# Clustered attention and a routed expert layer on one core: column groups, joint transposes, and sums moved off TensorE

## The chip, the cores and the metric

The kernel runs on one core of one Trainium2 chip. A core has TensorE (PE, matrix multiply; its weight loads are a row of their own, PEld), VectorE (DVE), ScalarE (ACT), GpSimd (POOL) and the queues that start transfers (SP is the queue of SyncE). The metric is the time of one execution on the device in microseconds (us). Before the change it is 852.24 us, the median of three runs (851.85 to 852.52).

## The reference

Two layers follow each other. The first is attention in clusters: queries and keys are assigned to the nearest of 16 centroids of their head, and a query sees only keys of its own cluster. The second sends each of 3072 rows to the one expert of 8 with the highest logit.

```python
# q, k, v: (4, 8, 768, 64); centroids: (8, 16, 64)
q_assign = argmax(q_n . c_n);  k_assign = argmax(k_n . c_n)          # per head
mask   = q_assign[:, :, :, None] == k_assign[:, :, None, :]
scores = where(mask, q @ k.T / sqrt(64), -1e9)
attn   = exp(scores - max);  attn = attn / (sum(attn) + 1e-9)
x      = (attn @ v) as rows (3072, 512)
# experts: w_gate (512, 8), w1 (8, 512, 1024), w2 (8, 1024, 512)
logits = x @ w_gate;  e = argmax(logits);  g = softmax(logits)[e]
out    = g * (relu(x @ w1[e]) @ w2[e])
```

## The kernel before

The kernel works on head pairs: 4 batches x 4 pairs = 16. A pair's queries and keys are turned (`turn`), compared with the centroids (`similar`, `similar2`), assigned (`assign`, `assign2`: one-hot rows), and the one-hots are turned too (`put`), so that a matmul of one-hots adds 0 where clusters agree and a huge negative number where they don't. Then come 12 units of scores and attention (`score`, `attend`) in two turns of six. Later `weigh` sums the exponentials and multiplies the attention result by the gate's matrix, `weigh2` turns both, `x_turn` writes the rows. The expert stage runs one group of rows per expert: whole tiles of 128 rows and one of 32.

```python
def put(g):                                       # one-hots of pair g, q and k apart
    ohT[g] = ohp.tile([P, 2, S], BF16, name="ohT")
    ps = ps_s.tile([P, 2, 512], F32, name="sps").bitcast(BF16)
    for w in range(2):
        for j in range(NQ):
            nc.tensor.transpose(  # L651
                ps[:, w, j * P : (j + 1) * P],
                ohs[:, (j % (NQ // 2)) * 4 + w * 2 + j // (NQ // 2)].rearrange("p a c -> p (a c)"), ident_b,
            )
    nc.scalar.copy(ohT[g][:, 0, :], ps[:, 0, 0:S])  # L655
    nc.vector.tensor_scalar(ohT[g][:, 1, :], ps[:, 1, 0:S], scalar1=BIG, scalar2=-BIG, op0=ALU.mult, op1=ALU.add)  # L656

def score(u):
    g, half, j = where(u)
    qs = slice(half * HS, (half + 1) * HS)
    ks = slice(j * P, (j + 1) * P)
    ps = ps_s.tile([P, 2, 512], F32, name="sps")
    for a in range(2):
        r = slice(a * D, (a + 1) * D)
        nc.tensor.matmul(ps[:, a, 0:HS], lhsT=qk[g][r, 1, ks], rhs=qk[g][r, 0, qs], start=True, stop=False)  # L673
    for a in range(2):
        r = slice(a * D, (a + 1) * D)
        nc.tensor.matmul(ps[:, a, 0:HS], lhsT=ohT[g][r, 1, ks], rhs=ohT[g][r, 0, qs], start=False, stop=True)  # L676
    A[u] = ap.tile([P, 2, HS], F32, name="A")
    nc.scalar.activation(A[u], ps[:, :, 0:HS], AF.Exp)  # L678

def weigh(g):                                     # sums and logits, two column groups of 32
    ps = ps_m.tile([P, 512], F32, name="mps")
    t = [T.pop((g, half)) for half in range(2)]
    for i in range(3):
        for half in range(2):
            nc.tensor.matmul(  # L711
                ps[half * 32 : (half + 1) * 32, 0:HS],
                lhsT=one_row[:, i, :] if i < 2 else wg[:, g % HP, :],
                rhs=t[half][:, i, :] if i < 2 else XT[g][:, half * HS : (half + 1) * HS],
                start=(i == 0), stop=(i == 2),
            )
    lsT[g] = stat.tile([64, HS], F32, name="lsT", bufs=1)
    nc.scalar.copy(lsT[g], ps[0:64, 0:HS])  # L718

def weigh2(g):
    lt = lsT.pop(g)
    ps = ps_m.tile([P, 512], F32, name="mps")
    for i in range(NQ // 2):
        nc.tensor.transpose(ps[:, i * 64 : (i + 1) * 64], lt[:, i * P : (i + 1) * P], ident[0:64, 0:64])  # L725
    ls = stat.tile([P, NQ, 32], F32, name="ls")
    nc.vector.tensor_copy(ls, ps[:, 0 : NQ * 32].rearrange("p (t r) -> p t r", r=32))  # L727
    den = ls[:, :, 2 * E : 2 * E + 2]
    # ...
```

The scaling in `turn`, and the order in which the parts stand (of a turn, part 0 comes between its six scores and its six attends, part 1 behind the attends; the scores of pair g begin in turn n = 2 g):

```python
def turn(g, piece):
    # ... transposes of queries and keys into ps (L599)
    if piece == 0:
        nc.vector.tensor_scalar_mul(flat[:, 0:S], ps[:, 0:S], D**-0.5)  # L603
        nc.scalar.copy(flat[:, S:1024], ps[:, S:1024])  # L604
    else:
        nc.scalar.copy(flat[:, 1024 : 2 * S], ps[:, 0 : 2 * S - 1024])  # L606

for g in range(NG):
    n = g * TG
    if g == 0:
        at(-4, 0, turn, g, 0)
        at(-4, 1, turn, g, 1)
        at(-3, 0, similar, g)
        at(-3, 1, similar2, g)
    elif g == 1:
        for f, a in ((turn, (g, 0)), (turn, (g, 1)), (similar, (g,)), (similar2, (g,))):
            at(-1 if f is similar2 else -2, 1, f, *a)
    else:
        at(n - 3, 0, turn, g, 0)
        at(n - 3, 0, turn, g, 1)
        at(n - 3, 1, similar, g)
        at(n - 2, 0, similar2, g)
    at(n - 2, 0, assign, g)
    at(n - 2, 0, assign2, g)
    at(n - 1, 0, put, g)
    at(n, 1, finish, g, 0)
    at(n + 1, 1, finish, g, 1)
    # ...
```

`similar` holds L613 (matmuls with the centroids) and L618, `similar2` L624 and L626, `assign` and `assign2` L632 to L641, `attend` L693, `finish` L701 (its result `xT`), `x_turn` L754 and L757.

The experts' second layer. The 32 rows use four column groups, each over a quarter of the 1024 inner elements, and a last matmul with `fold` (four identities of 32 on top of each other) adds the four parts; `rows_out` scales (L315) and scatters (L316) the rows. The first layer is L301, its evictions L309 and L311; L282 turns gathered rows.

```python
def layer2(g):
    zq = zc = None
    if g["n"][last] < P:
        zq = wide()
        n = FB * RQ // P
        for i in range(n):
            for t in range(P // RQ):
                nc.tensor.matmul(  # L334
                    zq[t * RQ : (t + 1) * RQ, 0, :], lhsT=g["h"][:, t * n + i, last * P : last * P + RQ],
                    rhs=g["w"][1][:, t * n + i, :], start=(i == 0), stop=(i == n - 1),
                )
        zc = p1.tile([P, Dm], F32, name="zo", bufs=3)
        nc.vector.tensor_copy(zc, zq[:, 0, :])  # L339
    for j, m in enumerate(g["n"]):
        if m < P:
            continue
        zp = wide()[:, 0, :]
        for fb in range(FB):
            nc.tensor.matmul(  # L345
                zp, lhsT=g["h"][:, fb, j * P : (j + 1) * P], rhs=g["w"][1][:, fb, :],
                start=(fb == 0), stop=(fb == FB - 1),
            )
        rows_out(g, j, P, zp)
    if zc is not None:
        zf = wide()[0:RQ, 0, :]
        nc.tensor.matmul(zf, lhsT=fold, rhs=zc, start=True, stop=True)  # L352
        rows_out(g, last, RQ, zf)
```

At the end two questions are loaded and asked: whether more groups of rows are left than were unrolled, and whether the general path has to run. With these inputs neither does.

```python
nx = nc.values_load(xe[0:1, NX : NX + 1], min_val=0, max_val=NX)  # L1020
general = nc.values_load(xe[0:1, NX + 1 : NX + 2], min_val=0, max_val=1)  # L1021
with tc.If(nx > XU):  # L1022
    with tc.For_i(XU, nx, 1) as i:
        ex = nc.sync.value_load(xe[0:1, bass.ds(i, 1)], min_val=0, max_val=E - 1)
        # ...
mctx.close()
late.close()
with tc.If(general > 0):  # L1035
    in_general(tc, ident, ident_b, first_c, first_e, wpool, q, k, v, centroids, moe_w_gate, moe_w1, moe_w2, out)
```

Of the kernel before, what the change touches and what calls it, by code (L numbers as in the profile page):

```python
# [8 lines left out]
F32 = mybir.dt.float32  # L9
# [12 lines left out]
XU = 2  # L22
# [161 lines left out]
def kernel(  # L184
# [78 lines left out]


    def wide():
        return ps_s.tile([P, 2, 512], F32, name="sps")
# [46 lines left out]
    def rows_out(g, j, m, zp):  # L313
        zo = p1.tile([P, Dm], F32, name="zo", bufs=3)
# [10 lines left out]
    def layer2(g):  # L325
        last = len(g["n"]) - 1
        zq = zc = None
        if g["n"][last] < P:

            zq = wide()  # L330
            n = FB * RQ // P
            for i in range(n):
                for t in range(P // RQ):
                    nc.tensor.matmul(  # L334
                        zq[t * RQ : (t + 1) * RQ, 0, :], lhsT=g["h"][:, t * n + i, last * P : last * P + RQ],
                        rhs=g["w"][1][:, t * n + i, :], start=(i == 0), stop=(i == n - 1),
                    )
            zc = p1.tile([P, Dm], F32, name="zo", bufs=3)
            nc.vector.tensor_copy(zc, zq[:, 0, :])  # L339
# [10 lines left out]
        if zc is not None:  # L350
            zf = wide()[0:RQ, 0, :]
            nc.tensor.matmul(zf, lhsT=fold, rhs=zc, start=True, stop=True)  # L352
            rows_out(g, last, RQ, zf)
# [7 lines left out]
    fold = consts.tile([P, RQ], F32)  # L361
# [5 lines left out]
    def place_consts():  # L367
# [9 lines left out]

        for t in range(P // RQ):
            nc.gpsimd.tensor_copy(fold[t * RQ : (t + 1) * RQ, :], ident[t * RQ : (t + 1) * RQ, t * RQ : (t + 1) * RQ])
# [22 lines left out]
    xe = rte.tile([1, NX + 2], I32)  # L402
# [100 lines left out]
    with ExitStack() as actx:  # L503
        ld = actx.enter_context(tc.tile_pool(name="ld", bufs=2))
        qkp = actx.enter_context(tc.tile_pool(name="qkp", bufs=2))
        ohp = actx.enter_context(tc.tile_pool(name="ohp", bufs=2))
# [37 lines left out]
        nc.vector.tensor_copy(ident_b, ident)  # L544
        first_c = iota("first_c", [P, C], [[-1, C]], C, 0)
        first_e = iota("first_e", [P, E], [[-1, E]], E, 0)

        wg = consts.tile([P, DB, 32], F32)
        nc.gpsimd.memset(wg, 0.0)
        one_row = consts.tile([P, 2, 32], F32)  # L550
        nc.gpsimd.memset(one_row, 0.0)
        for a in range(2):
            r = slice(a * D, (a + 1) * D)
            nc.gpsimd.tensor_copy(wg[r, :, a * E : (a + 1) * E], wg_in[r])
            nc.gpsimd.memset(one_row[:, a, 2 * E + a : 2 * E + a + 1], 1.0)

        ohs = consts.tile([P, 2 * NQ, 2, D], BF16, name="oh")
        nc.gpsimd.memset(ohs, 0.0)

# [31 lines left out]
        def turn(g, piece):  # L591
# [9 lines left out]
            if piece == 0:  # L601

                nc.vector.tensor_scalar_mul(flat[:, 0:S], ps[:, 0:S], D**-0.5)  # L603
# [33 lines left out]
        def assign2(g):  # L637
# [3 lines left out]
            nc.vector.tensor_tensor(  # L641
                ohs[:, :, :, 0:C], rank.rearrange("p (t a) c -> p t a c", a=2),
                top.rearrange("p (t a) -> p t a", a=2).unsqueeze(3).to_broadcast([P, 2 * NQ, 2, C]), op=ALU.is_equal,
            )

        def put(g):
            ohT[g] = ohp.tile([P, 2, S], BF16, name="ohT")
            ps = ps_s.tile([P, 2, 512], F32, name="sps").bitcast(BF16)
            for w in range(2):
                for j in range(NQ):  # L650
                    nc.tensor.transpose(  # L651
                        ps[:, w, j * P : (j + 1) * P],
                        ohs[:, (j % (NQ // 2)) * 4 + w * 2 + j // (NQ // 2)].rearrange("p a c -> p (a c)"), ident_b,
                    )
            nc.scalar.copy(ohT[g][:, 0, :], ps[:, 0, 0:S])  # L655
            nc.vector.tensor_scalar(ohT[g][:, 1, :], ps[:, 1, 0:S], scalar1=BIG, scalar2=-BIG, op0=ALU.mult, op1=ALU.add)  # L656
# [49 lines left out]
        def weigh(g):  # L706
            ps = ps_m.tile([P, 512], F32, name="mps")
            t = [T.pop((g, half)) for half in range(2)]
            for i in range(3):
                for half in range(2):  # L710
                    nc.tensor.matmul(  # L711
                        ps[half * 32 : (half + 1) * 32, 0:HS],
                        lhsT=one_row[:, i, :] if i < 2 else wg[:, g % HP, :],
                        rhs=t[half][:, i, :] if i < 2 else XT[g][:, half * HS : (half + 1) * HS],
                        start=(i == 0), stop=(i == 2),
                    )
            lsT[g] = stat.tile([64, HS], F32, name="lsT", bufs=1)
            nc.scalar.copy(lsT[g], ps[0:64, 0:HS])  # L718

        def weigh2(g):  # L720
# [3 lines left out]
            for i in range(NQ // 2):  # L724
                nc.tensor.transpose(ps[:, i * 64 : (i + 1) * 64], lt[:, i * P : (i + 1) * P], ident[0:64, 0:64])  # L725
            ls = stat.tile([P, NQ, 32], F32, name="ls")
            nc.vector.tensor_copy(ls, ps[:, 0 : NQ * 32].rearrange("p (t r) -> p t r", r=32))  # L727
            den = ls[:, :, 2 * E : 2 * E + 2]
# [3 lines left out]

            lgh = stat.tile([P, NQ, 2, E], F32, name="lgh")
            nc.vector.tensor_tensor(
                lgh, ls[:, :, 0 : 2 * E].rearrange("p t (a e) -> p t a e", a=2),
# [59 lines left out]
        for g in range(NG):  # L795
# [6 lines left out]
            elif g == 1:  # L802

                for f, a in ((turn, (g, 0)), (turn, (g, 1)), (similar, (g,)), (similar2, (g,))):
                    at(-1 if f is similar2 else -2, 1, f, *a)
# [107 lines left out]
    with tc.tile_pool(name="sm", bufs=1) as sm:  # L913
# [54 lines left out]
        xe_f = sm.tile([1, NX + 2], F32)  # L968
# [7 lines left out]
        nc.vector.tensor_tensor(xe_f[:, NX : NX + 1], ove[0:1, E - 1 :], bad[0:1, 3:4], op=ALU.mult)  # L976
# [88 lines left out]
```

## Time and profile before

| | |
|---|---|
| median of three runs | 852.24 us |
| span in the profile | 849.3 us |
| mean granted TensorE clock | 0.995 |
| instructions | 10767 |
| attention: scores begin to be complete | 22.83 us |
| one head pair, in the steady part | 24.8 us |
| expert stage with gathered rows, first matmul | 467.89 us |
| last matmul starts | 837.70 us |

A profile is one execution. Its page gives the busy time of each engine, the chain of work that ended last, and groups of instructions: source line, engine, operation, output <- inputs, shape, how often, busy time, mean ns of one, and the idle time just before them with what ended it. The timeline gives the same instructions in order of time: start, length, engine, line, how many were merged, and in brackets the idle time of the engine before them. Line numbers are those of the kernel before. A 32-bit matmul stands there as two records; a 32-bit transpose and a bf16 matmul as one. The length of a matmul's record includes time in the pipeline, so two neighbours overlap; what a block of matmuls costs is the distance from its start to the start of the next block.

In the stages, of 100 us from 200 to 300 (attention) PE is busy 100.0, DVE 65.2, ACT 52.9 and POOL 5.4; of 100 us from 600 to 700 (experts) PE 100.0, DVE 8.9, ACT 12.0 and POOL 15.9.

### The profile page before, as it was taken

The numbers are of one execution on the slowest core, as the hardware profiler recorded it, in microseconds if no ns is written. First come the engines' busy times: TensorE is split into PE (matmuls) and PEld (weight loads), VectorE is DVE, ScalarE is ACT, GpSimd is POOL, SyncE is SP. The second block draws the span as 40 slices with busy tenths as digits, with TensorE's granted clock in tenths as the row PEclk, the third lists the DMA queues.
The fourth block names the chain that finished last, engine by engine and source line by source line (L and its number), as shares of the span: only waits on it lengthen the run. The fifth ranks groups of instructions, "written<-read, shape, count | busy, mean of one in ns | idle before, by whom it ended". The sixth has DMA issues, their size and how long they took to land.

```text
span 849.3 us, 10767 instructions
## 1 busy us (share of the span) xinstructions
PE 820.6 (97%) x4397; PEld 435.6 (51%) x4397; DVE 320.5 (38%) x559; ACT 264.0 (31%) x406; POOL 106.2 (13%) x165
## 2 busy tenths in 40 slices
PE   4999999999999999999999999999999999999994
PEld 2544455454455555454666655645454444545472
DVE  3566666675666566786452101001001010101000
ACT  3554555555455455545311111111011111110010
POOL 2200000000000000011024020211020303020010
PEclk9999999999999999999999999999999999999998
DMA  9027321272242102201332243443242424321010
GB/s 206 1 57 239 72 56 56 77 254 56 57 131 57 37 21 57 94 1 39 137 150 63 73 173 137 150 163 117 112 140 112 166 100 160 119 69 70 25 39 7
DMA packets 76186, 81.69 MB, mean 96 GB/s; under 512 B 52831, under 2 KB 56927, under 8 KB 75616
## 3 DMA queue, kind: packets, MB, share of 16 engines
q1 hardware_dynamic: 70208, 60.82, 23.6%
q0 software_dynamic: 5248, 20.04, 6.4%
q8 instruction: 37, 0.61, 0.3%
q14 instruction: 21, 0.17, 0.1%
q10 hardware_dynamic: 672, 0.05, 0.1%
HBM read 68.26 MB, written 13.68 MB: 96 GB/s over the span
## 4 chain that ended last, share of the span: by engine, by line
PE 48%; issue 39%; POOL 8%; DVE 3%; ACT 1%; DMA 0%; POOLq 0%; ACTq 0%; DVEq 0%
PE sps L673 14%; PE O L693 14%; PE mps L711 4%; PE sps L676 3%; POOL out_dram L316 3%; POOL xg L270 3%; PE sps L599 2%; PE sps L613 2%; PE sps L754 2%; PE sps L301 2%; PE sps L651 1%; POOL oh_c L468 1%; PE sps L624 1%; PE sps L345 1%; DVE T L685 1%
## 5 line engine op out<-in xcount | busy, mean ns | idle before, releaser
L301 PE MATMUL sps<-xgT,w 128*128 128x416 f32 (+2 forms) x640 | 175.2, 434 | 1.1 <-ACT xgT L290 1.1
L678 ACT ACTIVATE A<-sps 128x768 f32<-128x768 f32 x192 | 153.1, 811 | 50.2 <-PE sps L676 48.9
L345 PE MATMUL sps<-w,h_sb 128*128 128x512 f32 x368 | 160.6, 595 | 1.3 <-DVE h_sb L309 0.9
L673 PE MATMUL sps<-qk 64*128 64x384 f32 x768 | 158.6, 491 | 0.0
L301 PEld LDWEIGHTS sps<-xgT,w 128*128 128x128 f32 x640 | 111.1, 190 | 67.5 <-issue 49.8
L309 DVE TENSOR_SCALAR h_sb<-sps 128x416 f32<-128x416 f32 (+2 forms) x34 | 18.7, 550 | 316.6 <-PE sps L301 316.6
L693 PE MATMUL O<-A,v_in 128*64 128x384 f32 x768 | 130.9, 490 | 0.0
L685 DVE TENSOR_TENSOR T<-T,A 128x768 f32<-128x768 f32 x128 | 122.7, 958 | 13.8 <-DVE T L681 0.5
L345 PEld LDWEIGHTS sps<-w,h_sb 128*128 128x128 f32 x368 | 69.1, 190 | 91.7 <-issue 85.6
L673 PEld LDWEIGHTS sps<-qk 64*128 64x128 f32 x768 | 66.6, 187 | 47.7 <-issue 41.2
L693 PEld LDWEIGHTS O<-A,v_in 128*64 128x64 f32 x768 | 52.3, 137 | 62.7 <-issue 62.6
L315 ACT ACTIVATE zo<-sps,xg 128x512 f32<-128x512 f32 (+1 forms) x34 | 23.3, 685 | 180.0 <-PE sps L345 171.0
L316 POOL DMA_INDIRECT out_dram<-zo,s_idx x34 | 33.0, 969 | 319.0 <-ACT zo L315 316.1
L311 ACT ACTIVATE h_sb<-sps 128x416 f32<-128x416 f32 (+2 forms) x34 | 16.5, 485 | 162.7 <-DVE h_sb L309 162.7
L676 PE MATMUL sps<-ohT 64*128 64x384 bf16 x384 | 63.2, 323 | 0.3 <-DVE ohT L656 0.3
L634 POOL TENSOR_TENSOR sim<-sim,first_c 128x384 f32<-128x384 f32 x16 | 16.0, 998 | 270.3 <-DVE sim L633 270.3
L681 DVE SCALAR_TENSOR_TENSOR T<-A 128x768 f32<-128x768 f32 x32 | 30.6, 958 | 49.0 <-ACT A L678 49.0
L701 ACT COPY xT<-O 128x384 f32<-128x384 f32 x32 | 15.4, 483 | 73.6 <-PE O L693 73.6
L270 POOL DMA_INDIRECT xg<-x_rows,g_idx x34 | 32.8, 964 | 20.1 <-issue 9.8
L676 PEld LDWEIGHTS <-ohT 64*128 64x128 bf16 x384 | 19.3, 94 | 25.5 <-DVE ohT L656 0.9
L757 DVE TENSOR_TENSOR x<-sps,rd 128x384 f32<-128x384 f32 x32 | 17.6, 553 | 28.4 <-PE sps L754 28.4
L711 PE MATMUL mps<-T,one_row 128*32 128x384 f32 x128 | 23.8, 492 | 0.0
(191 smaller groups left out, 534.0 us busy)
## 6 DMA issues: line engine op xcount, KB each, us to landing
w<-in_moe_w_dram SPq DMA_DIRECT2D x20, 2048.0 KB, 8.8
x_rows<-x POOLq DMA_DIRECT2D x4, 1548.0 KB, 7.2
q_in<-in_q_dram SPq DMA_DIRECT2D x32, 192.0 KB, 4.5
k_in<-in_k_dram SPq DMA_DIRECT2D x32, 192.0 KB, 4.7
v_in<-in_v_dram SPq DMA_DIRECT2D x16, 384.0 KB, 3.3
xg<-x_rows,g_idx POOLq DMA_INDIRECT x34, 5.5
out_dram<-zo,s_idx POOLq DMA_INDIRECT x34, 2.9
csb<-in_centroids_dram ACTq DMA_DIRECT2D x1, 32.0 KB, 1.7
```

Of the source, the lines that this page charges most:

```text
L270: nc.gpsimd.indirect_dma_start(out=g["xg"][0:m, j, :], out_offset=None, in_=x_d[0 : g["rows"], :], in_offset=bass.IndirectOffsetOnAxis(ap= ...
L301: nc.tensor.matmul(o, lhsT=g["w"][0][:, c, fb * P : (fb + 1) * P], rhs=g["xT"][:, c, :cols], start=(c == 0), stop=(c == DB - 1),)
L315: nc.scalar.activation(zo[0:m], zp[0:m], AF.Copy, scale=g["xg"][0:m, j, Dm : Dm + 1])
L316: ins = nc.gpsimd.indirect_dma_start(out=out[:, :], out_offset=bass.IndirectOffsetOnAxis(ap=g["si"](j)[0:m], axis=0), in_=zo[0:m], in_offs ...
L345: nc.tensor.matmul(zp, lhsT=g["h"][:, fb, j * P : (j + 1) * P], rhs=g["w"][1][:, fb, :], start=(fb == 0), stop=(fb == FB - 1),)
L673: nc.tensor.matmul(ps[:, a, 0:HS], lhsT=qk[g][r, 1, ks], rhs=qk[g][r, 0, qs], start=True, stop=False)
L676: nc.tensor.matmul(ps[:, a, 0:HS], lhsT=ohT[g][r, 1, ks], rhs=ohT[g][r, 0, qs], start=False, stop=True)
L678: nc.scalar.activation(A[u], ps[:, :, 0:HS], AF.Exp)
L681: nc.vector.scalar_tensor_tensor(T[g, half], in0=A[u - 1], scalar=1e-9 / P, in1=A[u], op0=ALU.add, op1=ALU.add)
L685: nc.vector.tensor_tensor(T[g, half], T[g, half], A[u], op=ALU.add)
L693: nc.tensor.matmul(O[g, half][a * D : (a + 1) * D, 0:HS], lhsT=rows[g, "v"][:, a, j, :], rhs=a_[:, a, :], start=(j == 0), stop=(j == NQ - 1),)
L711: nc.tensor.matmul(ps[half * 32 : (half + 1) * 32, 0:HS], lhsT=one_row[:, i, :] if i < 2 else wg[:, g % HP, :], rhs=t[half][:, i, :] if i ...
```

## The change

Five things are changed at once.

1. Sums and logits in four column groups. `weigh` used three matmuls for each of two column groups, with both heads' sums and logits in the same 32 columns. Now each half and head has a column group of its own, with two matmuls. The result fills 128 partitions instead of 64.
2. Joint one-hot transposes. Queries' and keys' one-hots stand side by side in 128 columns, so one transpose turns both: 6 instead of 12. The keys' part is then taken from other partitions by two operations on 16 partitions each. Rows that no key fills are set to 0 once, in two fixed buffers.
3. The 32-row sums leave TensorE: `fold` and its matmul go; ScalarE copies three of the four parts, VectorE adds them.
4. One question at the end: a value computed earlier says whether either of the two paths is needed.
5. Another order of the first turns: pair 1's similarities come a turn later, so that they no longer stand before pair 0's one-hot transposes, ScalarE scales pair 1's queries, and 12 matmuls of the identity run at the start, before any data is there.

```diff
 def layer2(g):
...
+            zc = pools["wk"].tile([RQ, P // RQ, Dm], F32, name="zc", bufs=1)
+            for t in range(1, P // RQ):
+                nc.scalar.copy(zc[:, t, :], zq[t * RQ : (t + 1) * RQ, :])
+            nc.vector.tensor_tensor(zc[:, 0, :], zc[:, 1, :], zq[0:RQ, :], op=ALU.add)
+            for t in range(2, P // RQ):
+                nc.vector.tensor_tensor(zc[:, 0, :], zc[:, 0, :], zc[:, t, :], op=ALU.add)
+            rows_out(g, last, RQ, zc[:, 0, :])
...
-        if zc is not None:
-            zf = wide()[0:RQ, 0, :]
-            nc.tensor.matmul(zf, lhsT=fold, rhs=zc, start=True, stop=True)
-            rows_out(g, last, RQ, zf)
...
-        for t in range(P // RQ):
-            nc.gpsimd.tensor_copy(fold[...], ident[...])
...
+        ps = ps_m.tile([P, 512], F32, name="mps")
+        for i in range(12):
+            nc.tensor.matmul(ps[:, 0:P], lhsT=ident, rhs=ident, start=True, stop=True)
...
-        ohs = consts.tile([P, 2 * NQ, 2, D], BF16, name="oh")
+        ohs = ohp.tile([P, NQ, 2, 2, 32], BF16, name="oh")
         nc.gpsimd.memset(ohs, 0.0)
+        ohTs = []
+        for i in range(2):
+            t = ohp.tile([P, 2, S], BF16, name=f"ohT{i}")
+            nc.gpsimd.memset(t[:, 1, :], 0.0)
+            ohTs.append(t)
...
 def turn(g, piece):
-                nc.vector.tensor_scalar_mul(flat[:, 0:S], ps[:, 0:S], D**-0.5)
+                if g == 1:
+                    nc.scalar.mul(flat[:, 0:S], ps[:, 0:S], D**-0.5)
+                else:
+                    nc.vector.tensor_scalar_mul(flat[:, 0:S], ps[:, 0:S], D**-0.5)
...
 def assign2(g):                                  # the comparison is cut in two, for q and for k
...
 def put(g):
+            oh = ohT[g] = ohTs[g % 2]
+            ps = wide()[:, 0, :].bitcast(BF16)
+            for j in range(NQ):
+                nc.tensor.transpose(
+                    ps[:, j * P : (j + 1) * P],
+                    ohs[:, (j % (NQ // 2)) * 2 + j // (NQ // 2)].rearrange("p a w c -> p (a w c)"), ident_b,
+                )
+            nc.scalar.copy(oh[:, 0, :], ps[:, 0:S])
+            for a in range(2):
+                nc.vector.tensor_scalar(
+                    oh[a * D : a * D + C, 1, :], ps[a * D + 32 : a * D + 32 + C, 0:S],
+                    scalar1=BIG, scalar2=-BIG, op0=ALU.mult, op1=ALU.add,
+                )
...
 def weigh(g):
-            for i in range(3):
+            for i in range(2):
                 for half in range(2):
+                    for a in range(2):
+                        r = (2 * half + a) * 32
+                        nc.tensor.matmul(
+                            ps[r : r + 32, 0:HS], lhsT=wg[:, g % HP, a, :] if i else one_row,
+                            rhs=XT[g][:, half * HS : (half + 1) * HS] if i else t[half][:, a, :],
+                            start=(i == 0), stop=(i == 1),
+                        )
+            lsT[g] = stat.tile([P, HS], F32, name="lsT", bufs=1)
+            nc.scalar.copy(lsT[g], ps[:, 0:HS])
...
 def weigh2(g):
-                nc.tensor.transpose(ps[:, i * 64 : (i + 1) * 64], lt[:, i * P : (i + 1) * P], ident[0:64, 0:64])
+                nc.tensor.transpose(ps[:, i * P : (i + 1) * P], lt[:, i * P : (i + 1) * P], ident)
...
             elif g == 1:
-                for f, a in ((turn, (g, 0)), (turn, (g, 1)), (similar, (g,)), (similar2, (g,))):
-                    at(-1 if f is similar2 else -2, 1, f, *a)
+                at(-2, 1, turn, g, 0)
+                at(-2, 1, turn, g, 1)
+                at(-1, 1, similar, g)
+                at(0, 0, similar2, g)
...
+    more = nc.values_load(xe[0:1, NX + 2 : NX + 3], min_val=0, max_val=2)
+    with tc.If(more > 0):
+        nx = nc.values_load(...)
+        general = nc.values_load(...)
+        with tc.If(nx > XU):
+            # ... as before
+        with tc.If(general > 0):
+            # ... as before
```

## The prediction

> **What bounds the kernel now.** I read the page first, its busy shares and its chain of waits.
>
> ```profile
> PE 820.6 (97%) x4397; PEld 435.6 (51%) x4397; DVE 320.5 (38%) x559; ACT 264.0 (31%) x406; POOL 106.2 (13%) x165
> ...
> PE 48%; issue 39%; POOL 8%; DVE 3%; ACT 1%; DMA 0%; POOLq 0%; ACTq 0%; DVEq 0%
> ```
>
> PE (TensorE) is busy 97% and nothing else is over 38%; in the chain PE leads too, and its "issue" share is time in which GpSimd's queue (the line after the experts' outputs) merely stood behind PE's own pace. But a matmul's end is modelled, so I don't count gains in busy time. I count in start-to-start distances on PE: from the first matmul of a block to the first matmul of the block after it. Those tile the time without overlap. The groups of instructions, kept apart by shape, give how often each block stands; for the fold:
>
> ```profile
> L352 PE MATMUL sps<-zo,fold 128*32 128x512 f32 x16 | 8.4, 605 | 0.0
> ```
>
> A 32-bit matmul leaves two records, so these 16 are 8 folds; likewise the 192 records of L711 are 96 matmuls, 6 for each of 16 head pairs. What a block costs PE is read in PE's timeline of one pair:
>
> ```profile
> 224.58 1.48 PE L711 MATMUL mps<-T,one_row 128*32 128x384 f32 x8
> 225.89 0.81 PE L711 MATMUL mps<-xT,wg 128*32 128x384 f32 x4
> 226.64 0.55 PE L624 MATMUL sps<-ident,simT 128*128 128x128 f32 x3
> ...
> 236.99 0.84 PE L651 MATMUL sps<-ident_b,oh 128*128 128x128 bf16 x12
> 237.67 0.82 PE L599 MATMUL sps<-ident,q_in 128*128 128x128 f32 x6
> ...
> 243.58 0.90 PE L613 MATMUL sps<-qk,cblk 128*32 128x384 f32 x8
> 244.40 0.59 PE L673 MATMUL sps<-qk 64*128 64x384 f32 x2
> ```
>
> The sums and logits take 224.58 to 226.64 (2.06 us), the one-hot transposes 236.99 to 237.67 (0.68). One pair's scores start at 219.53, the next one's of the same half at 244.40: 24.87 us, with no hole on PE. In the expert stage the same view shows a fold and its surroundings:
>
> ```profile
> 486.69 14.00 PE L345 MATMUL sps<-w,h_sb 128*128 128x512 f32 x32
> 500.63 1.04 PE L352 MATMUL sps<-zo,fold 128*32 128x512 f32 x2
> 501.60 15.79 PE L301 MATMUL sps<-xgT,w 128*128 128x288 f32 x64
> ```
>
> And the beginning, where PE does wait, with long holes:
>
> ```profile
> 13.48 0.82 PE L599 MATMUL sps<-ident,k_in 128*128 128x128 f32 x6
> 17.96 2.29 PE L613 MATMUL sps<-qk,cblk 128*32 128x384 f32 x8 [3.66 <-DVE qk L603]
> 20.19 1.16 PE L651 MATMUL sps<-ident_b,oh 128*128 128x128 bf16 x12
> ...
> 22.83 0.34 PE L676 MATMUL sps<-ohT 64*128 64x384 bf16 x2 [0.30 <-DVE ohT L656]
> ```
>
> The first scores are complete only from 22.83 us on, because PE's queue has pair 1's similarities (L613) ahead of pair 0's one-hot transposes (L651), and these similarities wait for a scaling (L603) that stands on VectorE behind pair 0's assignment.
>
> [...] the similarities (L613) use four column groups; their 8 records at 243.58 take 0.82 us to the next block, 0.78 in the median of 14, which is two steps of 0.32 (a 384-column record alone; the attends, two column groups, come 24 records in 4.02 us, 0.335 a step of two)[...]. [...] the transposes at 7.09 come 0.21 us apart, those at 12.83 0.11, and the clock record falls to half again from 17.5 to 20.9 us, after the hole from 14.3. [...] So an operation on 16 or 32 partitions costs what 128 cost. Trace: 1x176 in 324 ns beside 128x176 in 341; ScalarE's 32x512 in 678 beside 128x512 in 688. [...] Trace: one compare-and-branch of PE at the end took 3.34 us, one of GpSimd 45 ns.
>
> **The change, part by part.**
>
> *Sums and logits.* Before, 6 matmuls in two column groups are 12 records, 6 steps of 0.32 and 0.13: 2.06, as measured. After, 8 matmuls in four groups are 16 records in 4 steps: 4 x 0.32 + 0.13 = 1.42. 0.64 a pair, x16 = **-10.3**. The result now fills 128 partitions, so the transposes after it read 128 columns instead of 64: 3 x 0.053 more. [...] I put this at 0 to 0.15 a pair, **+0.5** in all. The copies read as many columns as before or fewer.
>
> *Joint one-hot transposes.* 12 become 6 at 0.057 (0.68 / 12): -0.34 a pair, **-5.4**. Not free elsewhere: VectorE's mask, one of 0.55 us, becomes two on 16 partitions of 0.55 each, started 0.47 apart, and the comparison is cut in two, about +0.1.
>
> *32-row sums off TensorE.* From the last layer-2 matmuls to the fold are 13.93 for 32 records of 0.429[...]; then 0.98 to L301: 1.19. Where no fold stands (816.05 to 823.00, 16 records) 0.08 is left over. So -1.1, x8 = **-8.8**. The new work is three ScalarE copies (0.68 each) and three VectorE additions (about 0.7): some 4 us, during the 13.9 to 20.8 us of the 128-row tiles, on engines at 10 to 13% there. Hidden. The PSUM tile is held about 3 us longer, but is the oldest of three and wanted again only after two 6.9 us tiles.
>
> *First turns.* Pair 0's transposes move ahead of pair 1's similarities, and ScalarE scales pair 1. New chain: GpSimd's memsets grow by some 0.7 us (three of 768 bf16 for one of 1536, 1.38), so the centroid block is ready near 7.5 and not 6.85; 12 identity matmuls (24 cold records of 0.21, 5.1 us from 1.5) end near 6.6, just before PE is first wanted at 6.85, and leave it warm: the first transposes halve. Scaling about 8.0 instead of 9.04, the assignment near 16.1 instead of 16.95. Then transposes (0.5), ScalarE's copy (0.8), two masks (1.0): first complete score near 18.8, 4.0 earlier. Against it: 0.48 for pair 1's similarity transposes, which now stand inside the first turns, and perhaps 0.5 of cold clock when the scores start. **-3.0**. In pair 0's second turn PE waits 1.75 us (44.13) for a chain that GpSimd's constants hold up; the four fold copies (0.94) leave it, one mask (0.47) joins: **-0.5**.
>
> *The end.* GpSimd loads the second question at 841.60, branches, and starts its 6.03 us drain at 842.43, after which the program ends. Without it the drain can start some 0.7 earlier: **-0.7**.
>
> *What is given back.* Three pairs carry the gate's softmax, and there the similarities start just as ScalarE's copy ends:
>
> ```profile
> 143.63 0.59 ACT L606 COPY qk<-sps 128x512 f32<-128x512 f32 x1
> ...
> 144.22 0.20 PEld L613 LDWEIGHTS sps<-qk,cblk 128*32 128x32 f32 x8 [0.17 <-ACT qk L606]
> ```
>
> The mask's 0.47 and PE's own 0.34 lead come to 0.8, of which the first half of the similarities (0.32) can cover some: 0.5 x 3 = **+1.5**. In the other pairs that chain has about 1.4 us in hand (in one the copy starts at 67.72 and takes 0.59, and the similarities start at 69.74), of which 0.6 stays.
>
> Sum: -10.3 + 0.5 - 5.4 - 8.8 - 3.0 - 0.5 - 0.7 + 1.5 = -26.7, so 825.5; I say **826 us** (-3.1%).
>
> **Rivals.** (a) Four column groups with two different moving operands don't run abreast, and the sums stay at 6 to 8 steps: 0 to +10 us there, the whole at 836 to 847. Against it: the similarities already feed four groups with four different operands. (b) VectorE becomes the bound of a pair: it has 65 us busy in 100, 16.2 of 24.8; after +0.6 it is 16.8 of 23.9, 70%. It can only bind where the chain mask, scaling, copy, similarities is late. If it were late in all 14 pairs by 0.5, +5.5: 832. (c) The 32-row path stalls: ScalarE works in order and waits for the additions; if the next tile's eviction or a PSUM buffer waited, PE would lose up to 1 us x8: 834. For it speaks only that the tile is held longer. (d) The start gains nothing as the loads or the cold clock set it: 829.
>
> **Range and chances.** The first three terms (-24.5) come from equal blocks measured in this trace; I trust them to 3 us. The start may be anything from 0 to -5, the gate pairs 0 to +3, the end 0 to -1. Together 820.5 to 831.5 for 8 in 10. For less than 2% (835.2 and up) a rival like (a) must hold: 5%. Slower by over 2% has no mechanism I can find: 1%.
>
> **What would show it.** The sums block should be 1.4 start to start, the one-hot block 0.34, the pair's period 23.9; L301 should follow L345 within 0.1; the first mask-completed score near 19; GpSimd's drain near 6 us. A pair's period over 24.3 with a hole before the similarities would show (b); a hole before L301 or in the 128-row tiles (c). I'm wrong if the sums block stays near 2 us.

## The result, and the profile after

| | before | after |
|---|---|---|
| median | 852.08 us (851.85 to 852.52, 4 runs) | 828.27 us (828.12 to 829.10, 4 runs) |
| ratio, with its 95% interval | | 0.9722 [0.9705, 0.9739] |
| span in the profile | 849.3 us | 827.1 us |
| last matmul starts | 837.70 us | 816.00 us |
| from there to the end of the span | 11.6 us | 11.1 us |

The change brings 23.8 us, 2.8%. The prediction was 826 us.

The line numbers move with the change. Those used below: one-hot transposes L651, now L665; the copy behind them L655, now L670; the mask L656, now L672; turn L599, now L607; scaling L603, now L614 (L612 for pair 1); its copies L604 and L606, now L615 and L617; similarities L613, now L624; scores L673 and L676, now L692 and L695; attends L693, now L712; sums L711, now L733; their transposes L725, now L746; `x_turn` L754, now L778; first expert layer L301, now L303; second L345, now L352. In the experiments the numbers move by a few lines more; operands and shapes tell which is which.

The page after, busy shares and chain of waits:

```profile
PE 802.3 (97%) x4373; PEld 431.8 (52%) x4373; DVE 340.0 (41%) x607; ACT 277.4 (34%) x431; POOL 106.2 (13%) x162
...
PE 45%; issue 39%; POOL 8%; DVE 5%; ACT 1%; POOLq 0%; ACTq 0%; DVEq 0%
```

TensorE is still what bounds it, but DVE (VectorE) has grown from 3 to 5% of the chain. That is a first hint at a new wait, and PE's timeline of one pair shows it (start, length, engine, line, operands, how many records, in brackets the idle time before):

```profile
216.50 0.85 PE L733 MATMUL mps<-T,one_row 128*32 128x384 f32 x8
217.17 0.83 PE L733 MATMUL mps<-xT,wg 128*32 128x384 f32 x8
217.93 0.55 PE L635 MATMUL sps<-ident,simT 128*128 128x128 f32 x3
...
228.28 0.51 PE L665 MATMUL sps<-ident_b,oh 128*128 128x128 bf16 x6
228.62 0.82 PE L607 MATMUL sps<-ident,q_in 128*128 128x128 f32 x6
...
234.19 0.52 PE L778 MATMUL sps<-ident,xT 128*128 128x128 f32 x3
235.49 1.33 PE L624 MATMUL sps<-qk,cblk 128*32 128x384 f32 x8 [0.78 <-ACT qk L615]
236.74 0.92 PE L692 MATMUL sps<-qk 64*128 64x384 f32 x4
```

The sums take 216.50 to 217.93, 1.43 us (predicted 1.42). The one-hot block takes 0.34, as predicted. But from 234.19 to 236.74 `x_turn` takes 1.30 and the similarities 1.25. In the same turn of the kernel before, the similarities ran from 243.58 to 244.40 (0.82, shown in the prediction), and `x_turn` started 0.48 ahead of them:

```profile
243.10 0.55 PE L754 MATMUL sps<-ident,xT 128*128 128x128 f32 x3
```

PE now waits for ScalarE's copy L615, and then once more for L617 in the middle of the similarities. The turn shown is one of those with the gate's softmax. In the expert stage nothing is left between the layers; 13.84 us lead from L352 to L303, where 13.93 and a fold of 0.98 stood:

```profile
474.52 14.00 PE L352 MATMUL sps<-w,h_sb 128*128 128x512 f32 x32
488.36 4.04 PE L303 MATMUL sps<-xgT,w 128*128 128x288 f32 x16
```

And the beginning. The timeline of PE first, then busy times by stretch (from:to, length, busy time and number of instructions of PE, PEld, DVE, ACT, POOL, then the granted PE clock, the share of the DMA engines and GB/s):

```profile
12.44 0.82 PE L607 MATMUL sps<-ident,k_in 128*128 128x128 f32 x6
16.02 0.82 PE L665 MATMUL sps<-ident_b,oh 128*128 128x128 bf16 x6 [2.77 <-DVE oh L655]
16.77 1.51 PE L624 MATMUL sps<-qk,cblk 128*32 128x384 f32 x8
18.21 1.65 PE L692 MATMUL sps<-qk 64*128 64x384 f32 x4
19.65 0.53 PE L695 MATMUL sps<-ohT 64*128 64x384 bf16 x2
...
21.25 0.53 PE L695 MATMUL sps<-ohT 64*128 64x384 bf16 x2
```

```profile
13.20:15.40 2.20, 0.05 (x1) 0.00 (x0) 1.05 (x3) 1.22 (x3) 0.99 (x1) 1.00 1.36 218
15.50:18.90 3.40, 2.88 (x16) 1.27 (x18) 1.59 (x5) 0.80 (x1) 0.00 (x0) 0.50 1.24 264
18.90:22.30 3.40, 3.40 (x16) 1.72 (x14) 0.54 (x1) 1.29 (x2) 0.00 (x0) 0.50 0.49 79
```

The first complete score starts at 19.65 instead of 22.83. But the clock is at half rate from 15.5 to 22.3 us (before: 17.5 to 20.9), so the block from scores to masked scores takes 1.44 and 1.28 us instead of 0.64 to 0.76. By the first scores of the second turn (31.15 before, 29.76 after) 1.4 of the 3.2 us are left: the half rate takes 1.3, and pair 1's similarity transposes, which now stand inside this turn, take 0.48.

### The profile page after: what moved, and what is told of

The parts are those of the page before. It is cut to its first block, busy times and chain, and to the rows that moved or that the text cites. A ratio compares the mean times of both kernels' runs of the same rounds, so it can differ in the third digit from the quotient of the medians.

```text
span 827.1 us, 10778 instructions
## 1 busy us (share of the span) xinstructions
PE 802.3 (97%) x4373; PEld 431.8 (52%) x4373; DVE 340.0 (41%) x607; ACT 277.4 (34%) x431; POOL 106.2 (13%) x162
## 3 DMA queue, kind: packets, MB, share of 16 engines
q1 hardware_dynamic: 70208, 60.82, 24.5%
## 4 chain that ended last, share of the span: by engine, by line
PE 45%; issue 39%; POOL 8%; DVE 5%; ACT 1%; POOLq 0%; ACTq 0%; DVEq 0%
PE sps L692 15%; PE O L712 14%; POOL out_dram L318 4%; PE sps L695 4%; POOL xg L272 3%; PE mps L733 3%; PE sps L624 2%; DVE T L704 2%; PE sps L303 2%; PE sps L607 2%; PE sps L778 1%; POOL oh_c L467 1%; PE sps L635 1%; PE mps L746 1%; PE sps L352 1%
## 5 line engine op out<-in xcount | busy, mean ns | idle before, releaser
L303 PE MATMUL sps<-xgT,w 128*128 128x416 f32 (+2 forms) x640 | 174.3, 433 | 1.5 <-issue 1.5
L352 PE MATMUL sps<-w,h_sb 128*128 128x512 f32 x368 | 160.6, 595 | 1.2 <-DVE h_sb L311 0.8
L692 PE MATMUL sps<-qk 64*128 64x384 f32 x768 | 160.4, 496 | 0.1
L303 PEld LDWEIGHTS sps<-xgT,w 128*128 128x128 f32 x640 | 111.8, 190 | 65.0 <-issue 55.3
L712 PE MATMUL O<-A,v_in 128*64 128x384 f32 x768 | 130.9, 490 | 0.0
L352 PEld LDWEIGHTS sps<-w,h_sb 128*128 128x128 f32 x368 | 69.1, 190 | 91.5 <-issue 85.5
L692 PEld LDWEIGHTS sps<-qk 64*128 64x128 f32 x768 | 66.9, 189 | 50.1 <-issue 42.3
L712 PEld LDWEIGHTS O<-A,v_in 128*64 128x64 f32 x768 | 52.3, 137 | 62.4 <-issue 62.3
L695 PE MATMUL sps<-ohT 64*128 64x384 bf16 x384 | 63.6, 325 | 0.0
L317 ACT ACTIVATE zo<-sps,xg 128x512 f32<-128x512 f32 x26 | 17.9, 687 | 132.3 <-PE sps L352 123.3
L720 ACT COPY xT<-O 128x384 f32<-128x384 f32 x32 | 15.4, 483 | 63.9 <-PE O L712 63.9
L695 PEld LDWEIGHTS <-ohT 64*128 64x128 bf16 x384 | 19.5, 95 | 25.3 <-issue 0.6
L615 ACT COPY qk<-sps 128x256 f32<-128x256 f32 x16 | 5.9, 372 | 50.6 <-DVE qk L614 50.6
```

The costliest lines, as they stand in the source:

```text
L303: nc.tensor.matmul(o, lhsT=g["w"][0][:, c, fb * P : (fb + 1) * P], rhs=g["xT"][:, c, :cols], start=(c == 0), stop=(c == DB - 1),)
L352: nc.tensor.matmul(zp, lhsT=g["h"][:, fb, j * P : (j + 1) * P], rhs=g["w"][1][:, fb, :], start=(fb == 0), stop=(fb == FB - 1),)
L712: nc.tensor.matmul(O[g, half][a * D : (a + 1) * D, 0:HS], lhsT=rows[g, "v"][:, a, j, :], rhs=a_[:, a, :], start=(j == 0), stop=(j == NQ - 1),)
```

## The experiments

Twelve kernels ran. The kernel before was timed beside them (medians 851.95 to 852.25 us). Where a profile is compared, the distances are start to start on PE.

**One part at a time, added to the kernel before.** Which parts bring what they were thought to bring?

*Column groups alone* (`weigh`, `weigh2`, their weights).

```diff
-            for i in range(3):
-                for half in range(2):
+            for i in range(2):
+                for half in range(2):
+                    for a in range(2):
+                        r = (2 * half + a) * 32      # a column group for each half and head
```

> The kernel before with the sums and logits in four column groups and nothing else of the change. My theory: TensorE is the bound, the block goes from 2.06 to 1.43 us in 16 pairs and the transposes after it don't grow: -10.1 us against the kernel before, about 842. Rival: part of it is taken back by a wait elsewhere in the pair (VectorE or ScalarE): -5 to -8.

Measured: 841.93 us (841.19 to 842.45), ratio 0.9879 [0.9863, 0.9896], -10.3. As expected.

*32-row sums alone* (ScalarE copies, VectorE adds, no fold).

```diff
-            zf = wide()[0:RQ, 0, :]
-            nc.tensor.matmul(zf, lhsT=fold, rhs=zc, start=True, stop=True)
+            for t in range(1, P // RQ):
+                nc.scalar.copy(zc[:, t, :], zq[t * RQ : (t + 1) * RQ, :])
+            # ... three additions on VectorE
```

> The kernel before with the 32-row sums off TensorE and nothing else of the change. My theory: 1.08 us for each of 8 groups and 0.1 more in the first layer behind it (-9.4), and the four constant copies that leave GpSimd shorten pair 0's wait by up to 0.9: -9.4 to -10.3 us, about 842. Rival: ScalarE's and VectorE's new work delays an eviction: less than -8.

Measured: 841.88 us (840.93 to 842.14), ratio 0.9881 [0.9864, 0.9897], -10.4. As expected. Part of it is pair 0's second turn, where attends and wait take 4.83 instead of 5.84 us: GpSimd no longer makes `fold`.

*Order of the first turns alone*, with the 12 identity matmuls and ScalarE's scaling of pair 1.

```diff
-                for f, a in ((turn, (g, 0)), (turn, (g, 1)), (similar, (g,)), (similar2, (g,))):
-                    at(-1 if f is similar2 else -2, 1, f, *a)
+                at(-2, 1, turn, g, 0)
+                at(-2, 1, turn, g, 1)
+                at(-1, 1, similar, g)
+                at(0, 0, similar2, g)
```

> The kernel before with the other order of the first turns and the 12 identity matmuls, and nothing else of the change. My theory: the first complete score comes 3 to 4 us earlier, but the scores then start while the clock is at half rate, so that the second turn starts only 1.4 us earlier; with pair 0's wait -1.4 to -1.8 us, about 850.5. Rival (my prediction): the half clock costs 0.5 us at most and the gain is 3.0 to 3.5, about 848.8.

Measured: 847.01 us (846.89 to 848.89), ratio 0.9947 [0.9931, 0.9964], -5.2, more than either theory said. In its profile the first turns run at full rate (the similarities at 16.89 take 0.85 us, where those at 16.77 in the changed kernel take 1.51 at half rate); the first complete score is at 18.45, and pair 1's first scores come at 41.30 instead of 45.70. So the order is worth about 4 us where the clock holds.

*Joint transposes alone.*

```diff
-            for w in range(2):
-                for j in range(NQ):
-                    nc.tensor.transpose(ps[:, w, j * P : (j + 1) * P], ...)
+            for j in range(NQ):
+                nc.tensor.transpose(ps[:, j * P : (j + 1) * P], ...)   # q and k side by side
-            nc.vector.tensor_scalar(ohT[g][:, 1, :], ps[:, 1, 0:S], ...)
+            for a in range(2):
+                nc.vector.tensor_scalar(oh[a * D : a * D + C, 1, :], ps[a * D + 32 : a * D + 32 + C, 0:S], ...)
```

> The kernel before with the joint one-hot transposes and nothing else of the change. My theory: TensorE gains 0.34 us in 16 pairs (-5.4), but the second mask delays the scaling on VectorE by 0.5 us, so that TensorE waits 0.8 us before the similarities in the three pairs with the gate's softmax (+2.4) and some 0.8 more in pair 0: about -2.2 us, 850. Rival: the second mask is hidden everywhere: -5.4, 846.7.

Measured: 853.66 us (851.97 to 854.32, 14 runs), ratio 1.0015 [1.0007, 1.0024]: +1.4, slower. The expectation missed by 3.6. The one-hot blocks do fall from 0.68 to 0.34, 5.3 in all. Against that stand, in four turns, 0.55 to 0.60 before the similarities and 0.43 to 0.48 inside them, 4.1 together, and in pair 0's second turn 1.1 of wait and, at half clock from 45.1 to 48.6 us, 1.2 in the similarities and the first scores behind it. Three of the four turns are those in which the gate's softmax runs (of pairs 3, 7 and 11); the fourth, which the expectations below call pair 14's, is pair 13's second turn, in which the experts' rows begin to be chosen. They are called the four turns from here on.

The four differences sum to -24.5, the whole change, which has the one question besides, is -23.8: three of the four parts carry it. What remained was why the joint transposes bring nothing, and what the clock takes.

**Why the joint transposes bring nothing.** All engines in one of the four turns, in the changed kernel:

```profile
136.04 1.12 DVE L672 TENSOR_SCALAR ohT<-sps 16x768 bf16<-16x768 bf16 x2
...
137.19 0.96 DVE L614 TENSOR_SCALAR qk<-sps 128x768 f32<-128x768 f32 x1
...
137.54 0.55 PE L778 MATMUL sps<-ident,xT 128*128 128x128 f32 x3
...
138.18 0.37 ACT L615 COPY qk<-sps 128x256 f32<-128x256 f32 x1 [2.18 <-DVE qk L614]
138.45 0.59 ACT L617 COPY qk<-sps 128x512 f32<-128x512 f32 x1
...
138.61 1.33 PE L624 MATMUL sps<-qk,cblk 128*32 128x384 f32 x8 [0.52 <-ACT qk L615]
139.09 0.14 PEld L624 LDWEIGHTS sps<-qk,cblk 128*32 128x32 f32 x4 [0.34 <-ACT qk L617]
```

Two masks of 0.56, on 16 partitions each, stand on VectorE in front of the next pair's scaling; the one mask on 128 partitions took 0.55 before (L656, mean of 16). Behind the scaling ScalarE makes two copies one after the other; the similarities need the first for their first half and the second for their other half. Before, this chain ended exactly when PE arrived. Now it starts 0.57 later while PE arrives 0.34 earlier.

*Taken back in the changed kernel* (the diff above, reversed).

> The changed kernel with the joint one-hot transposes taken back (12 transposes and one mask again, the rest as changed). What the prediction held: the joint transposes bring 5.4 us and cost 1.5 in the gate's pairs and 0.5 of pair 0's wait, so without them the time rises by about 3, to 831.5. Theory now, from the first four runs: the mask cut in two stands on VectorE in front of the next pair's scaling, and in four pairs (3, 7, 11 and 14) and at pair 0 the whole delay of about 1.0 us reaches TensorE, 4.2 to 6 us, so the gain is eaten and without them the time stays or falls, 826.3 to 828.5. By blocks of TensorE's timeline: one-hot block 0.68 again, the wait before the similarities of the four pairs gone.

Measured: 827.10 us (825.56 to 827.74), against 828.12 to 829.10 with joint transposes. The theory's range holds, the prediction's 831.5 doesn't. By blocks: one-hots +5.1; the four turns -4.4; pair 0's attends and wait 4.35 instead of 5.21; the first scores -1.0, since the clock is at half rate for 3.4 us instead of 6.8; an expert group's turn of rows -0.45 (see the end). The last two aren't shown to belong to the transposes; without them gain and loss are even, to within some tenths.

*The masks behind the scaling*, in the changed kernel.

```diff
-            for a in range(2):                    # in put(g)
-                nc.vector.tensor_scalar(oh[...], ps[...], ...)
+            put_ps[g] = ps
+        def mask(g):
+            oh, ps = ohT[g], put_ps.pop(g)
+            for a in range(2):
+                nc.vector.tensor_scalar(oh[...], ps[...], ...)
...
                 at(n - 3, 0, turn, g, 1)
+                at(n - 3, 0, mask, g - 1)
...
+            if g in (0, NG - 1):
+                at(n - 1, 0, mask, g)
```

> The changed kernel with one thing moved: the two masks of pair g-1 go to VectorE behind the scaling of pair g, which TensorE's similarities wait for. Theory (the masks' place is what eats the gain): the four waits of 1.03 us before the similarities go, and about 1 us of pair 0's, so 828.3 falls by 4 to 5, to 823.3 to 824.3. Rival (the waits come from ScalarE's copy or the gate's own operations on VectorE): no change in those pairs, 828. Second rival: the PSUM buffer that the masks read is freed some 1 us later and the next user waits: part of the gain back.

Measured: 822.55 us (822.34 to 822.78), ratio to the kernel before 0.9656 [0.9643, 0.9669]; -5.7 in the medians with one move. The same place in the same turn:

```profile
133.83 0.92 DVE L614 TENSOR_SCALAR qk<-sps 128x768 f32<-128x768 f32 x1
...
134.78 1.12 DVE L676 TENSOR_SCALAR ohT<-sps 16x768 bf16<-16x768 bf16 x2
134.78 0.37 ACT L615 COPY qk<-sps 128x256 f32<-128x256 f32 x1 [0.85 <-DVE qk L614]
135.05 0.59 ACT L617 COPY qk<-sps 128x512 f32<-128x512 f32 x1
135.47 0.55 PE L783 MATMUL sps<-ident,xT 128*128 128x128 f32 x3
...
135.94 0.85 PE L624 MATMUL sps<-qk,cblk 128*32 128x384 f32 x8
```

The masks now lie beside ScalarE's copies, and the similarities follow 0.48 behind `x_turn` with nothing in between. All four turns lose their wait (-4.5), pair 0's attends and wait take 4.54 instead of 5.21, and the similarities behind them 1.26 instead of 1.57. The second rival, later freed buffers, shows only in pair 14: its first masked scores are followed 0.65 later instead of 0.16, by a wait for a PSUM buffer that VectorE reads late (L786):

```profile
353.76 0.92 PE L697 MATMUL sps<-qk 64*128 64x384 f32 x4 [0.32 <-DVE x L786]
```

Together, with pair 14's loss taken off, that is -4.9, inside the -4 to -5 of the theory. The profiles differ by 6.5, because the start is 1.1 shorter (half rate for 3.4 us instead of 6.8) and the expert group's turn 0.45 shorter in this one. Neither is shown to come from the move, so some 5 us are what the move is worth, and how much of the rest is in the 5.7 of the medians stays open.

*The masks behind the scaling, but the transposes apart again.* Does the joint form bring its gain once nothing waits for it?

```diff
+            for w in range(2):
+                for j in range(NQ):
+                    nc.tensor.transpose(ps[:, w, j * P : (j + 1) * P], ...)
+        def mask(g):
+            nc.vector.tensor_scalar(ohT[g][:, 1, :], put_ps.pop(g)[:, 1, 0:S], ...)   # one mask
```

> The changed kernel with the masks behind the scaling and the joint transposes taken back (12 transposes and one mask). Theory: with the masks out of the way the joint transposes bring what their block shows, 16 x 0.34 = 5.4 us less at most 0.6 at pair 0, so this kernel takes 822.55 + 4.8 to 5.4, about 827.5, the same as without the joint transposes and with the mask in its old place (827.1). Rival: the new place of the mask is worth as much to the single mask, and joint transposes bring nothing, 822.5 to 824.

Measured: 826.81 us (825.40 to 827.27): joint transposes bring 4.3 here, a little under the theory's 4.8 to 5.4, of 5.7 that their blocks show in the two traces. In the traces 0.45 of the 4.3 is the expert group's turn again, longer in this one. And the mask's place brings nothing to the single mask (827.10 and 826.81). So the two parts need each other.

*The gate's softmax half a turn later.* Its small operations on VectorE stand before the masks, in three of the four turns.

```diff
-                    at(n + 3, 0, gate, g // HP)
+                    at(n + 3, 1, gate, g // HP)
```

> The changed kernel with the gate's softmax moved half a turn later, nothing else. Theory: in pairs 3, 7 and 11 the softmax's seven small operations (about 1.4 us from first to last) stand in front of the masks and the scaling; without them there the 1.03 us wait goes in these three, -3.1, to 825.2; the fourth pair (14, where the choice of rows begins) keeps its wait, and pair 0 its own. Rival (masks alone are too much): the waits stay in part.

Measured: 824.60 us (823.46 to 825.59), -3.7. The waits with a softmax are gone (0.48 for `x_turn` and 0.78, once 0.88, for the similarities), the fourth turn keeps its own (1.10 and 1.26), as expected. In the profiled run the clock also stayed full at the start (granted 1.00 from 15.5 to 22.3 us, 0.50 in the changed kernel) and the expert group's turn is 0.45 shorter, which can account for the rest. One new wait: the transposes of pair 12's sums come 0.35 later.

**The clock at the start.** *12 more identity matmuls in PE's hole from 13.1 to 16.0 us.*

```diff
+        def stay_warm():
+            ps = ps_m.tile([P, 512], F32, name="mps")
+            for i in range(12):
+                nc.tensor.matmul(ps[:, 0:P], lhsT=ident, rhs=ident, start=True, stop=True)
...
+                at(-2, 1, stay_warm)
```

> The changed kernel with 12 more identity matmuls behind pair 1's turn, in TensorE's hole from 13.1 to 16.0 us. Theory (the half clock from 15.5 to 22.3 us is what kept the first turns from bringing their whole gain): the clock stays at full rate, the first complete score comes near 18.5 instead of 19.65 and the second turn's first scores near 27.3 instead of 29.76, -1.5 to -2.4 in the profile, to about 826. Rival (the one-hot chain on VectorE and ScalarE sets the start, not the clock): 828.

Measured: 826.59 us, -1.7, and the five runs lie within 0.4 (826.50 to 826.93) where the changed kernel's four lie within 1.0. PE's timeline, and one of the stretches of above:

```profile
13.09 2.84 PE L622 MATMUL mps<-ident 128*128 128x128 f32 x24
16.04 0.51 PE L670 MATMUL sps<-ident_b,oh 128*128 128x128 bf16 x6
16.48 0.85 PE L629 MATMUL sps<-qk,cblk 128*32 128x384 f32 x8
17.26 0.92 PE L697 MATMUL sps<-qk 64*128 64x384 f32 x4
18.02 0.33 PE L700 MATMUL sps<-ohT 64*128 64x384 bf16 x1
```

```profile
15.50:18.90 3.40, 3.04 (x26) 1.42 (x27) 1.90 (x5) 0.80 (x1) 0.00 (x0) 1.00 1.24 262
```

The one-hot transposes start at the same time as without them (16.04 and 16.02), so VectorE's chain sets that start; what follows up to the second turn is the clock. The first complete score comes at 18.02, the second turn's first scores at 27.41 instead of 29.76; 0.27 of that comes back as a longer wait in pair 0's second turn.

*Without the 12 identity matmuls at the very start.*

```diff
-        for i in range(12):
-            nc.tensor.matmul(ps[:, 0:P], lhsT=ident, rhs=ident, start=True, stop=True)
```

> The changed kernel without the 12 identity matmuls at the start. By the prediction the first 12 transposes come cold again, 3.05 instead of 2.19 us, and all that follows to the first scores moves by 0.9: 829.2, first complete score 20.5. Rival: the clock's half rate then ends later, or falls elsewhere, and the time stays or falls, 827.5 to 828.3.

Measured: 829.34 us (828.97 to 830.04), +1.1, first complete score 20.29. The first transposes are at half rate again:

```profile
6.91 1.49 PE L603 MATMUL sps<-ident,q_in 128*128 128x128 f32 x6
8.19 1.49 PE L603 MATMUL sps<-ident,k_in 128*128 128x128 f32 x6
```

3.06 us for the two, against 2.19 with the identities.

**The end.** *Both questions asked, as before.*

```diff
-    more = nc.values_load(xe[0:1, NX + 2 : NX + 3], min_val=0, max_val=2)
-    with tc.If(more > 0):
     # ... the two questions, one level further out
```

> The changed kernel with both questions asked at the end as before. From the start of the last matmul to the end of the span it takes 11.1 us in the changed kernel and 11.6 in the one before: +0.5, 828.8, with the distance back at 11.6. Rival (the distance comes from something else than the question): 828.3 and 11.1.

Measured: 828.08 us (827.15 to 829.74), so the median doesn't resolve it. The traces do: from the start of the last matmul to the end of the span 11.6 us, against 11.1. In the seven other runs with one question the distance is 11.1 as well, in the others with two 11.6 to 11.9.

**All three together.** Masks behind the scaling, softmax half a turn later, identities in the hole: the edits of `mask_after`, `gate_later` and `stay_warm` above.

```diff
+                at(-2, 1, stay_warm)
+                at(n - 3, 0, mask, g - 1)
-                    at(n + 3, 0, gate, g // HP)
+                    at(n + 3, 1, gate, g // HP)
```

> The changed kernel with the masks behind the scaling, the gate's softmax half a turn later and the 12 identity matmuls in TensorE's hole. Theory: the masks' place already takes the whole wait of the gate's pairs, so the softmax's place adds nothing to it; the warm clock adds 1.4 to 1.7; 822.55 becomes 820.8 to 821.2. Rival: the softmax behind the masks collides with the sums' copy (0.35 in one pair when it was moved alone): 821.5.

Measured: 822.27 us (821.87 to 822.36), ratio to the kernel before 0.9650 [0.9637, 0.9663]. It is the fastest that ran, 6.0 below the changed kernel, but only 0.3 below the masks' move alone, and both expectations missed. The clock holds (first complete score 18.22 instead of 19.06), but 0.35 is lost again before the transposes of pair 12's sums, as when the softmax was moved alone, and 0.43 in the expert group's turn of rows, which differs from trace to trace (below). What the identities bring beside the moved masks without the softmax's move was not tried.

## Why the prediction was nearly right, step by step

| step | predicted | measured in the profiles |
|---|---|---|
| sums in column groups | -10.3 | -10.1 (2.06 to 1.43, x16) |
| transposes behind them | +0.5 | 0.0 (0.81 to 0.80 with the next block) |
| joint one-hot transposes | -5.4 | -5.3 (0.68 to 0.34) |
| 32-row sums | -8.8 | -9.4 |
| first turns | -3.0 | -1.4; -3.5 to -3.9 in the four traces whose clock held there |
| pair 0's wait | -0.5 | -0.6 |
| gate pairs | +1.5 | +4.4, in four turns |
| an expert group's turn of rows | none | +0.45 |
| the end | -0.7 | -0.5 |
| sum | -26.7 | -22.4; the spans differ by 22.2, the medians by 23.8 |

The three large terms came out within 0.6 because they were start-to-start distances of repeated blocks. "Hidden" for the 32-row path was right: no hole stands before L303 or in the 128-row tiles, and rival (c) falls. Rival (a) falls with the 1.43 us block. The pair's period is 23.86 outside the four turns (48.39 to 72.25 from sums to sums; predicted 23.9), so rival (b), late everywhere, falls too. But its mechanism is what the four turns show: there the chain of mask, scaling, copies and similarities is late, and the period is 24.9 to 25.3 in three of them, with the hole that the prediction named as its sign. Rival (d), a start that gains nothing, falls with the order alone (-5.2), but the clock it named did take part of the gain.

The 0.13 us beside the steps of 0.32, and the 0.2 by which 13.93 exceeds 32 records of 0.429 before the fold, are what the measured distances left over. What they consist of was not shown; carrying the 0.13 over to the new sums was the author's estimate, and 1.43 came where it gave 1.42. The +0.5 for the transposes behind them was an estimate too, and 0.0 came.

The term that failed is what is given back: "0.5 x 3 = +1.5". The 0.8 us of delay was somewhat small (1.0 measured in these turns). Two things in it were wrong. First, the similarities' first half can't cover any of it. The two halves run abreast: in the kernel before they start at 144.22 and 144.28, and the next block begins 0.77 after the second half's start (145.05). In the changed kernel the first half starts 0.49 ahead of the second (138.61 and 139.09), and still the next block begins 0.77 after the second half's start (139.86). So only the second half counts, and it waits for L617, which stands behind L615 on ScalarE. Its slack, from the end of the second copy to its start, was 0.05 us in these three turns of the kernel before, which the lines shown in the prediction said; 0.6 of wait before the block and 0.43 inside it make up the whole delay. Second, a fourth turn had only 0.15. In nine other turns the slack falls from 1.45 (once 1.35) to 0.32 (once 0.23), where the prediction let 0.6 stay: the chain is late in every turn, and nine of them hide it. VectorE's timeline in the fourth turn, after the change:

```profile
349.84 0.18 DVE L455 CAST rc<-rc_i 128x36 f32<-128x36 int32 x1
349.94 0.95 DVE L700 SCALAR_TENSOR_TENSOR T<-A 128x768 f32<-128x768 f32 x1
350.99 4.14 DVE L704 TENSOR_TENSOR T<-T,A 128x768 f32<-128x768 f32 x4
355.15 1.13 DVE L672 TENSOR_SCALAR ohT<-sps 16x768 bf16<-16x768 bf16 x2
356.31 0.96 DVE L614 TENSOR_SCALAR qk<-sps 128x768 f32<-128x768 f32 x1
```

The small operations of the rows' choice (L455 is the last) have pushed the additions of the exponentials together, without a pause, up to the masks. The prediction looked for the turns with a softmax instead of measuring every turn's slack. Together that is 2.9 us, more than the 2.3 us by which the time missed. That the miss is no larger is in part luck: by the spans the change brings 22.2, 4.5 short of the sum, but the profiled execution of the kernel before was a short one (851.04 us, median 852.08) and that of the changed kernel the longest of its four (829.10).

In the first turns the mechanism and the order were right (18.8 was predicted for the first complete score; 18.02 to 18.45 where the clock held, 19.65 in this profile). The term for the "cold clock", 0.5, was the author's estimate, and mis-sized: the half rate took 1.3 of the gain in this profile, and filling the hole brings 1.7 in the median. The end was mis-sized by 0.2.

## What to carry to other kernels

When an engine off the bound takes on work, look up what stands behind it in its queue, and put the new work behind what the bound waits for: here one such move was worth some 5 us, a fifth of the whole change. Measure the slack of each repetition: nine turns had about 1.45 us of it and four next to none, which an average hides. Where two halves ran abreast, an early start of one covered no delay of the other (0.77 us from the second half's start to the next block, before and after). A saving on the bound also makes it arrive earlier at its next wait, so gain and lost slack add up there.

## What the runs showed of the hardware

PE's hole before the one-hot transposes, 2.77 us idle in the changed kernel, was followed by the half rate in some executions and not in others. With that same hole the clock was at half rate for 6.83 us (changed kernel, 15.47 to 22.30 us), for 3.41 (masks moved), and not at all (softmax moved). The second turn's first scores come at 29.76, 28.67 and 27.45 us in these three.

The traces also show that the hole's length alone doesn't decide. From 13.2 to 15.4 us PE was busy for 0.05 us in the changed kernel and for 0.10 with the softmax moved; from 15.5 to 18.9 the one was granted half the clock, the other all of it (0.50 and 1.00). In the kernel before, the 3.42 us ahead of its half rate (14.05 to 17.47) held 0.25 us of PE's work (with its modelled ends), in the changed kernel (12.06 to 15.47) 1.19, while 8.64 to 12.06 there, at full clock and with full clock behind it, held 2.30. The half rate ended after 3.41 us with 2.92 of work in them in the kernel before (17.47 to 20.88); in the changed kernel it went on after 3.41 us with 2.86 (15.47 to 18.88) and ended after another 3.42, all of them busy. Two traces make no rule of this, and what decides isn't shown.

Filling the hole didn't plainly take away the spread: the runs lie within 0.4 and 0.5 us in the two kernels with it filled, and within 0.4 with it open and the masks moved.

A turn of gathered rows early in the expert stage takes 2.48 us in five traces, 2.72 to 2.75 in four and 2.92 to 2.96 in five, with the same instructions in it: 2.93 in the changed kernel, 2.48 with the masks moved or the softmax moved, 2.92 with both. In the changed kernel VectorE's copy of the 32 rows starts 0.77 us after its copy of the 128 rows has ended, with the masks moved right behind it. Each kernel was traced once, so whether the kernel or the execution decides isn't shown, and the cause stays open.
